# Block-causal attention and two feed-forward layers on one core: the order of weight conversions and token cuts is changed in five places

## The chip, the cores and the metric

The kernel runs on one core of a Trainium2 chip. The metric is the device time of one execution in microseconds (us). Three runs of the kernel before gave 957.68 us in the median (956.08 to 958.67). The engines are named as the profile names them: PE multiplies matrices (PEld loads its weights), DVE and ACT do elementwise work, POOL helps in attention, SP issues DMAs. Each engine works through its own instructions in the order in which they were written.

## The reference

```python
# q, k, v: (4, 8, 576, 64); 2304 tokens of 512 after the heads are joined
scores = scale * q @ k^T;  mask by blocks of 64 (block_i >= block_j)
attn = softmax(scores);    x = (attn @ v), heads joined -> (2304, 512)
g = relu(x @ w_in) ** 2;   x = g @ w_out          # first layer, 512 -> 2048 -> 512
h = x @ w_in2;  g = h * cos(h);  out = g @ w_out2  # second layer, same sizes
```

## The kernel before, in words

**Number format.** Every fp32 operand of the two layers is held as two parts, "high" (the value rounded, made by ACT) and "low" (the rest, made by DVE from the value and the high part). A product of two such operands is three matmuls: high by high, high by low, low by high. Tokens are cut in this way by a copy and a subtraction. Weights come from DRAM as 64-bit words, and the class `Half` converts half a chunk (512 KB: a chunk's in-weights, h = 0, or its out-weights, h = 1) by eight instructions: on ACT `shift`, `rebias`, `high`, on DVE `mask`, `join`, `sign`, `power`, `low`. A call of `convert()` finishes one half, begins the next and asks SP to load a further one. The list `loads` sets the order of the halves.

**Stages.** Attention fills `xall` with all tokens. The order of its instructions is made by a planner, which also places the conversion of two halves (EARLY) and the cut of the first 512 tokens. The first layer then begins with a block of 768 tokens (512, and 256 beside them), in a loop over the 16 chunks of the hidden dimension, `first_block`: the hidden product of chunk c (24 matmuls), a conversion, ACT's activation of the chunk, its gs parts, a second conversion, and the output product of chunk c-1 (24 matmuls). The hidden product of chunk 1 is put into the banks `accs[3]` and `hs[3]`, which the output product of chunk 0 writes as its last ones. The in-weights are also written back to DRAM, and come again as "streams" (`ws`) for later blocks.

Three blocks of 512 tokens follow in the first layer (`first_layer`, eight steps r of two chunks each), and in the second layer four blocks of 512 tokens (`second_layer`, eight steps each) and a last one of 256 (`last_block`). A step's output matmuls are put in the list `pend`, and `pop` places them between later products, so that PE has work while DVE and ACT prepare the next operands.

**Second layer.** A hidden product is split into quarters and made from seven smaller products (42 matmuls of 256 columns), named by the weight part and the token part: 11 by 11, s2 by t2, s1 by t1, 12 by 21, s3 by t3, 22 by t4, s4 by 22. Their sums are taken on ACT (`copy`, into p1 and c11) and DVE (`plus`). The activation h·cos(h) of a step runs in pieces: `count`, `less`, `rest`, `size` at the step's end, `size`, `cosine`, `times`, `high`, `low` in the next step. For every block the tokens' quarters and their sums are prepared during the block before (`prepare`): four sums on DVE, and seven cuts, of which those of "11" and "t2" are the last. They are also the first two that the next block's products read. `prepared(n)` emits n of these items.

What the change touches: the sort key of `loads` (L234), the streams' ranges in `stream` (L827), the list that `prepare` returns (L974), the pops at the end of the first layer's last step (L1134), and in `second_layer` the places of `convert` and of `prepared` (L1187 to L1215).

Of the kernel before, what the change touches and what calls it, by code (L numbers as in the profile page):

```python
# [175 lines left out]
def tile_block_causal_attention__then__two_ffn(  # L176
# [54 lines left out]
    BESIDE = 256  # L231
    loads = [((layer, c), h) for layer in range(2) for c in range(KF) for h in range(2)]

    loads.sort(key=lambda x: (x[0][0], x[0][1] + (KF if x[0][0] else 1) * x[1], -x[1]))  # L234
    loads.reverse()
    loaded, begun = [], []
    freed, given, done = [0], [], set()
# [509 lines left out]
    def layers():  # L747
# [74 lines left out]
        def stream(s):  # L822
            i, r = steps[s]
            layer = blocks[i][0]
            assert layer == 0 or (layer, r, "sums", 1) in done
            w = ws_p.tile([128, 7 * DM], F32R, tag="ws", name="ws")
            ranges = [(0, 4)] if layer == 0 else [(0, 7)] if i < len(blocks) - 1 else [(0, 3), (7, 8)]  # L827
            at = 0
            for a, z in ranges:
                nc.sync.dma_start(  # L830
                    out=w[:, at * DM : (at + z - a) * DM].bitcast(F32), in_=parts[layer][r][:, a * DM : z * DM]
                )
                at += z - a
            return w
# [113 lines left out]
        def prepare(t0, n, own, room):  # L948

            m = 256  # L950
            src = {}
            def sum_of(name, one, two):
                if name in ("t1", "t2"):
                    tile = room(name == "t2")
                    for x, s in enumerate((name, "t3" if name == "t1" else "t4")):
                        src[s] = tile[:, x].rearrange("p (k n) -> p k n", k=2)[:, :, 0:m]
                nc.vector.tensor_tensor(out=src[name], in0=src[one], in1=src[two], op=ALU.subtract)

            def cut(name):
                to = own[name][:, :, :, 0:m]  # L960
                nc.scalar.copy(out=to[:, 0], in_=src[name])
                nc.vector.tensor_tensor(
                    out=to[:, 1], in0=src[name], in1=to[:, 0].bitcast(F32), op=ALU.subtract
                )

            if n == 256:
                src.update({name: xall[:, k : k + 2, t0 : t0 + n] for name, k in zip(names, (0, 2))})
                return [lambda name=name: cut(name) for name in names[0:2]]
            src.update({
                f"{k + 1}{j + 1}": xall[:, 2 * k : 2 * k + 2, t0 + j * m : t0 + (j + 1) * m]  # L970
                for k in range(2) for j in range(2)
            })
            sums = (("t1", "12", "11"), ("t3", "22", "12"), ("t2", "22", "t1"), ("t4", "21", "t2"))
            return [lambda s=s: sum_of(*s) for s in sums] + [lambda name=name: cut(name) for name in names]  # L974

        u = [x_p.tile([128, 256], F32, name=f"u{n}") for n in range(2)]

        place = {
# [119 lines left out]
        def pop(n):  # L1098
            for _ in range(min(n, len(pend))):
                pend.pop(0)()  # L1100
# [10 lines left out]
        def first_layer(s, i, r):  # L1111

            n, w, gs = blocks[i][2], ws.pop(0), gsb[s % 2]
            for x in range(2):
# [11 lines left out]
                if r < half - 1:  # L1126
                    pop(3 * KD)
                elif x:
                    if i < last:
                        fresh.extend(Cut(*blocks[i + 1][1:], kk) for kk in range(KD))  # L1130
                        for c in fresh:
                            c.high()
                            c.low()
                    pop(6 * KD)  # L1134
                squares(h, x, n, gs)
                if s == 0 and x == 0:
                    for a in range(KD):
# [20 lines left out]
                    prepared(1)  # L1158
            if i == last and r == half - 1:
                prepared(len(todo))  # L1160

        def second_layer(s, i, r):

# [6 lines left out]
            def copy(to, bank):  # L1170
                nc.scalar.copy(out=to, in_=bank[:, 0:m])  # L1171
# [12 lines left out]
            times("s1", "t1", bank_c, True)  # L1184
            times("12", "21", bank_a, False)
            copy(c11, bank_a)
            pop(2 if len(pend) > per else 0)  # L1187
            times("s3", "t3", bank_b, False)
            plus(c22, bank_b, p1)
            plus(c22, bank_c, c22)  # L1190
            run(("high", 1), ("low", 1), ("high", 0), ("low", 0))
            pop(len(pend) - per - 3)
            times("22", "t4", bank_b, False)
            plus(c21, bank_b, p1)
            pop(len(pend) - per)
            times("s4", "22", bank_c, False)
            plus(c12, bank_c, u2)
            late.clear()
            late.update(waves(n, gs, [ha[:, x, 0:n] for x in range(2)]))
            run(("count", 1), ("less", 1), ("count", 0), ("less", 0), ("rest", 1), ("rest", 0), ("size", 1))  # L1200
            ws.append(stream(s + 2))
            if loads or loaded or begun:
                convert()
            elif i + 1 < len(blocks):
                if r >= 1 and not todo and ready[0] < i:
                    ready[0] = i
                    if len(sets) < 2:
                        add_set()
                    todo.extend(prepare(
                        *blocks[i + 1][1:], sets[(i - last) % 2],  # L1210
                        lambda x: raw_p.tile([128, 2, 512], F32, tag="raw", name="t"),
                    ))
                prepared(max(0, min(2, len(todo) - 2)))
                if r == half - 1:
                    prepared(len(todo))  # L1215

        def last_block(s, i, r):

# [91 lines left out]
```

## Time and profile before

| what | us |
|---|---|
| median of three runs | 957.68 |
| the profiled execution | 955.75 |
| its span | 953.9 |
| PE busy in the span | 929.5 (97%) |
| DVE busy | 674.7 (71%) |
| ACT busy | 617.5 (65%) |

A row of the timeline has the start, the length, the engine, the line, the operation, what it writes and reads, and how many instructions were merged; in brackets stands the idle time before it and what ended it. The chain of waits is read in the same way, and a row of it shows the piece of the chain alone. A row of the windows view has the stretch, its length, the busy time of PE, PEld, DVE, ACT and POOL, then the granted TensorE clock as a share of full speed, the share of DMA and GB/s. Where a row's length is that of a group of matmuls, its end is modelled; the start of the next group tells when PE was free.

### The profile page before, as it was taken

The page shows a single profiled execution, that of the slowest core. Times are in us where ns is not written, and L with a number is a line of the kernel's source. Part 1 is how long each engine was busy: PE and PEld are TensorE (multiplying, and loading weights), DVE is VectorE, ACT ScalarE, POOL GpSimd, SP SyncE. Part 2 cuts the span into 40 slices and gives each one's busy share as a digit, 9 for nine tenths or more (in the row PEclk, how much of TensorE's full clock was granted, in tenths as well). Part 3 has the DMA queues.
Part 4 walks back from the last instruction along what each step waited for, and adds up shares of the span by engine and source line. Part 5 has one row for each costly group of instructions (what it writes and reads, how often), then busy time and mean ns, then how long its engine had stood idle before and what let it go on. Part 6 is the DMA issues. An engine that isn't in the chain of part 4 may idle for free.

```text
span 953.9 us, 15725 instructions
## 1 busy us (share of the span) xinstructions
PE 929.5 (97%) x5818; PEld 788.1 (83%) x5818; DVE 674.7 (71%) x1394; ACT 617.5 (65%) x1319; POOL 93.5 (10%) x204
## 2 busy tenths in 40 slices
PE   8999998999999999999999989999999999999998
PEld 4777776888888888888888878988998998998887
DVE  6998997777776556555466678767776876766554
ACT  7987897777886555655567765555555555544554
POOL 4867740000000000000000000000000000000000
PEclk9999999999999999999999999999999999999999
DMA  8444304567654777676555744446544555544272
GB/s 306 152 136 137 118 30 146 167 205 248 197 191 167 273 240 232 232 252 227 193 177 191 274 175 155 155 155 213 200 173 155 203 189 193 197 156 172 72 255 76
DMA packets 40156, 176.12 MB, mean 185 GB/s; under 512 B 4112, under 2 KB 9488, under 8 KB 32912
## 3 DMA queue, kind: packets, MB, share of 16 engines
q1 hardware_dynamic: 39360, 174.41, 52.9%
q8 instruction: 45, 0.74, 0.3%
q10 hardware_dynamic: 720, 0.72, 0.2%
q14 instruction: 31, 0.25, 0.1%
HBM read 145.23 MB, written 29.88 MB: 184 GB/s over the span
## 4 chain that ended last, share of the span: by engine, by line
PE 89%; DVE 4%; ACT 3%; DMA 2%; issue 1%; POOL 0%; ACTq 0%; SPq 0%; DVEq 0%
PE acc L1055 19%; PE h L988 16%; PE h L1119 14%; PE acc L1053 13%; PE h L855 5%; PE ps L656 4%; PE ps L440 4%; PE ps L601 4%; PE acc L879 4%; PE h L879 2%; PE h L1226 2%; DMA raw<-in_w_dram 1%; PE ps L488 1%; DVE g L1011 1%; PE ps L628 1%; DMA ws<-parts1.3_2028 1%
## 5 line engine op out<-in xcount | busy, mean ns | idle before, releaser
L1055 PE MATMUL acc<-w,gs 128*128 128x512 f32 x864 | 220.0, 392 | 0.0
L1055 PEld LDWEIGHTS acc<-w,gs 128*128 128x128 f32 x864 | 154.0, 189 | 25.3
L1053 PE MATMUL acc<-gs,w 128*128 128x512 f32 x576 | 138.3, 389 | 0.0
L1119 PE MATMUL h<-xs,ws 128*128 128x512 f32 x576 | 137.7, 389 | 0.0
L1119 PEld LDWEIGHTS h<-xs,ws 128*128 128x128 f32 x576 | 108.0, 188 | 22.3
L1053 PEld LDWEIGHTS acc<-gs,w 128*128 128x128 f32 x576 | 107.8, 188 | 22.2
L999 DVE TENSOR_TENSOR gs<-ha,gs 128x512 fp32r<-128x512 f32 x48 | 33.2, 692 | 91.7 <-ACT gs L998 91.7
L1008 ACT ACTIVATE turns<-ha 128x512 int32<-128x512 f32 x64 | 40.5, 633 | 73.7 <-DVE ha L1174 73.6
L1016 ACT ACTIVATE g<-g 128x512 f32<-128x512 f32 (+1 forms) x80 | 47.2, 590 | 52.7 <-DVE g L1011 52.7
L988 PE MATMUL h<-w,ws 128*128 128x256 f32 x480 | 70.8, 284 | 2.8 <-ACT u L1171 1.8
L1174 DVE TENSOR_TENSOR ha<-h,u 128x256 f32<-128x256 f32 x96 | 40.6, 423 | 45.3 <-PE h L988 45.2
L988 PEld LDWEIGHTS h<-w,ws 128*128 128x128 f32 x480 | 66.2, 192 | 7.6 <-ACT u L1171 2.2
L855 PE MATMUL h<-xs,w 128*128 128x256 f32 (+1 forms) x372 | 67.3, 336 | 1.2 <-ACT w L307 1.2
L307 ACT CAST w<-bits 128x512 fp32r<-128x512 f32 x64 | 39.9, 624 | 42.1 <-DVE bits L285 42.1
L855 PEld LDWEIGHTS h<-xs,w 128*128 128x128 f32 x372 | 57.9, 190 | 9.3 <-ACT w L307 1.4
L996 ACT ACTIVATE ha<-h 128x512 f32<-128x512 f32 x48 | 28.5, 594 | 52.4 <-PE h L1119 52.4
L1019 ACT ACTIVATE g<-g,half_pi 128x512 f32<-128x512 f32 (+1 forms) x80 | 50.6, 672 | 0.5
L1022 DVE TENSOR_TENSOR g<-ha,g 128x512 f32<-128x512 f32 x64 | 41.7, 692 | 12.0 <-ACT g L1019 11.8
L1028 DVE TENSOR_TENSOR gs<-g,gs 128x512 fp32r<-128x512 f32 (+1 forms) x80 | 47.9, 631 | 2.6 <-ACT gs L1025 2.5
L1011 DVE SCALAR_TENSOR_TENSOR g<-turns,g 128x512 f32<-128x512 int32 (+1 forms) x80 | 48.0, 633 | 0.5
L1011 DVE SCALAR_TENSOR_TENSOR g<-turns,ha 128x512 f32<-128x512 int32 x64 | 44.0, 688 | 5.1 <-ACT turns L1008 5.0
L656 PE MATMUL ps<-PT,vB 128*64 128x320 f32 (+4 forms) x448 | 46.8, 360 | 0.0
(173 smaller groups left out, 1693.3 us busy)
## 6 DMA issues: line engine op xcount, KB each, us to landing
raw<-in_w_dram SPq DMA_DIRECT2D x64, 512.0 KB, 4.4
qB<-in_qd_dram SPq DMA_DIRECT2D x15, 576.0 KB, 5.4
ws<-parts1.0_2025 SPq DMA_DIRECT2D x4, 1792.0 KB, 7.4
ws<-parts1.1_2026 SPq DMA_DIRECT2D x4, 1792.0 KB, 7.2
ws<-parts1.2_2027 SPq DMA_DIRECT2D x4, 1792.0 KB, 7.3
ws<-parts1.3_2028 SPq DMA_DIRECT2D x4, 1792.0 KB, 8.3
ws<-parts1.4_2029 SPq DMA_DIRECT2D x4, 1792.0 KB, 7.4
ws<-parts1.5_2030 SPq DMA_DIRECT2D x4, 1792.0 KB, 7.2
```

The lines of the kernel that those rows point to most:

```text
L656: nc.tensor.matmul(plan.bank(s)[own, a - c0 : c1 - c0], lhsT=vB[x][:, j, e], rhs=PT[:, x, j, e, a:c1], start=(n == 0), stop=(n == len(todo ...
L855: nc.tensor.matmul(h, lhsT=w[:, a, kk * 128 : (kk + 1) * 128], rhs=xs[kk].parts[:, y], start=(m == 0), stop=(m == 3 * KD - 1),)
L879: nc.tensor.matmul(accs[a][:, 0:n], lhsT=w[:, x, a * 128 : (a + 1) * 128], rhs=gs[:, y], start=(c == 0 and m == 0 and a % shared == 0), st ...
L988: nc.tensor.matmul(bank[:, 0:n], lhsT=w[:, c : c + 128], rhs=own[two][:, y, k, 0:n], start=(start and k == 0 and i == 0), stop=(k == 1 and ...
L1011: nc.vector.scalar_tensor_tensor(out=own, in0=turn, scalar=-part, in1=start, op0=ALU.mult, op1=ALU.add)
L1016: nc.scalar.activation(out=own, in_=own, func=AF.Abs)
L1019: nc.scalar.activation(out=own, in_=own, func=AF.Sin, bias=half_pi, scale=-1.0)
L1022: nc.vector.tensor_tensor(out=own, in0=h, in1=own, op=ALU.mult)
L1028: nc.vector.tensor_tensor(out=to[:, 1], in0=own, in1=to[:, 0].bitcast(F32), op=ALU.subtract)
L1053: nc.tensor.matmul(accs[a][:, 0:n], lhsT=w[:, y, sl], rhs=gs[:, z, x, 0:n], **flags)
L1055: nc.tensor.matmul(accs[a], lhsT=gs[:, y, x, sl], rhs=w[:, z], **flags)
L1119: nc.tensor.matmul(h[:, 0:n], lhsT=w[:, c : c + 128], rhs=xs[kk].parts[:, y], start=(m == 0), stop=(m == 3 * KD - 1),)
```

## The change

Five edits. The halves of the first layer's weights come in the order c + 1.5·h, so that the two converted in attention are the in-weights of chunks 0 and 1, and each chunk's out-weights come half a place after the next chunk's in-weights. The cuts of "11" and "t2" are split: both high parts, then both low parts. In the second layer the conversion moves from the step's end to its middle, the high parts of the last two cuts to the middle of the block's last step, and the low parts right behind its last sum. The first layer's last step pops 12 output matmuls instead of 24, and ends with a Sin on one column, which brings ACT's table load there. The last block's streams come in three DMAs instead of two.

```diff
-    loads.sort(key=lambda x: (x[0][0], x[0][1] + (KF if x[0][0] else 1) * x[1], -x[1]))
+    loads.sort(key=lambda x: (x[0][0], x[0][1] + (KF if x[0][0] else 1.5) * x[1]))
...
-            ranges = [(0, 4)] if layer == 0 else [(0, 7)] if i < len(blocks) - 1 else [(0, 3), (7, 8)]
+            ranges = [(0, 4)] if layer == 0 else [(0, 7)] if i < len(blocks) - 1 else [(0, 2), (2, 3), (7, 8)]
...
-            def cut(name):
+            def high(name):
+                nc.scalar.copy(out=own[name][:, 0, :, 0:m], in_=src[name])
+
+            def low(name):
                 to = own[name][:, :, :, 0:m]
-                nc.scalar.copy(out=to[:, 0], in_=src[name])
                 nc.vector.tensor_tensor(
...
+            def cut(name):
+                high(name)
+                low(name)
...
-            return [lambda s=s: sum_of(*s) for s in sums] + [lambda name=name: cut(name) for name in names]
+            return [lambda s=s: sum_of(*s) for s in sums] + [lambda name=name: cut(name) for name in names[0:5]] + [
+                lambda name=name, f=f: f(name) for f in (high, low) for name in names[5:]
+            ]
...
-                    pop(6 * KD)
+                    pop(6 * KD if i < last else 3 * KD)
...
                 prepared(len(todo))
+                nc.scalar.activation(out=scrap, in_=half_pi, func=AF.Sin)
...
             copy(c11, bank_a)
+            if r == half - 1:
+                prepared(2)
             pop(2 if len(pend) > per else 0)
...
             run(("high", 1), ("low", 1), ("high", 0), ("low", 0))
+            if loads or loaded or begun:
+                convert()
             pop(len(pend) - per - 3)
...
             plus(c12, bank_c, u2)
+            if r == half - 1:
+                prepared(len(todo))
...
-            if loads or loaded or begun:
-                convert()
-            elif i + 1 < len(blocks):
+            if not (loads or loaded or begun) and r < half - 1 and i + 1 < len(blocks):
...
-                prepared(max(0, min(2, len(todo) - 2)))
-                if r == half - 1:
-                    prepared(len(todo))
+                prepared(max(0, min(2, len(todo) - 4 * (blocks[i + 1][2] > 256))))
```

The first place is ACT at the beginning of the first layer, where w0 names in-weights, w1 out-weights, h0, h1 and acc3, h3 the banks of the hidden products of chunks 0 and 1. Before:

```order
L307 CAST w1_2000<-bits_1972 128x512
...
L866 CAST gs0_2036<-ha_2033 128x256
L261 ACTIVATE raw_1997<-raw_1997 128x512
L307 CAST w0_2108<-bits_2089 128x512
L274 ACTIVATE bits_2106<-bits_2106,new_bias_59 128x512
L261 ACTIVATE raw_2093<-raw_2093 128x512
L307 CAST w1_2144<-bits_2106 128x512
L274 ACTIVATE bits_2142<-bits_2142,new_bias_59 128x512
L864 ACTIVATE ha_2033<-acc3_2048 128x512
```

And now:

```order
L307 CAST w0_2000<-bits_1972 128x512
...
L866 CAST gs0_2036<-ha_2033 128x256
L261 ACTIVATE raw_1997<-raw_1997 128x512
L307 CAST w1_2108<-bits_2089 128x512
L274 ACTIVATE bits_2106<-bits_2106,new_bias_59 128x512
L261 ACTIVATE raw_2093<-raw_2093 128x512
L307 CAST w0_2144<-bits_2106 128x512
L274 ACTIVATE bits_2142<-bits_2142,new_bias_59 128x512
L864 ACTIVATE ha_2033<-acc3_2048 128x512
```

No instruction has moved: the same places of the conversion now hold other weights, w0_2000 being chunk 1's in-weights, w1_2108 chunk 0's out-weights and w0_2144 chunk 2's in-weights.

The second place is DVE at the end of the first layer (gs1 is the activation of its last step, w1 an out-weight's low part, x11 and xt2 the low parts of the cuts of "11" and "t2", u1 and ha the second layer's sums). Before:

```order
L962 TENSOR_TENSOR x11_4822<-xall_60,x11_4822 128x512
L999 TENSOR_TENSOR gs1_2037<-ha_2033,gs1_2037 128x512
L962 TENSOR_TENSOR xt2_4823<-turns_2035,xt2_4823 128x512
L999 TENSOR_TENSOR gs1_2037<-ha_2033,gs1_2037 128x512
L285 SCALAR_TENSOR_TENSOR bits_5198<-raw_5120,bits_5198 128x512
L268 TENSOR_SCALAR bits_5272<-raw_5162 128x512
L291 TENSOR_SCALAR raw_5120<-bits_5198 128x512
L310 SCALAR_TENSOR_TENSOR w1_5274<-raw_5120 128x512
L279 SCALAR_TENSOR_TENSOR raw_5162<-raw_5162 128x512
L1174 TENSOR_TENSOR u1_3352<-h1_2042,u0_3351 128x256
```

And now:

```order
L1008 TENSOR_TENSOR gs1_2037<-ha_2033,gs1_2037 128x512 x2
L285 SCALAR_TENSOR_TENSOR bits_5199<-raw_5121,bits_5199 128x512
L268 TENSOR_SCALAR bits_5259<-raw_5163 128x512
L291 TENSOR_SCALAR raw_5121<-bits_5199 128x512
L310 SCALAR_TENSOR_TENSOR w1_5261<-raw_5121 128x512
L279 SCALAR_TENSOR_TENSOR raw_5163<-raw_5163 128x512
L964 TENSOR_TENSOR x11_4823<-xall_60,x11_4823 128x512
L964 TENSOR_TENSOR xt2_4824<-turns_2035,xt2_4824 128x512
L1184 TENSOR_TENSOR u1_3353<-h1_2042,u0_3352 128x256
```

Both low parts now stand behind the last gs and behind all five DVE instructions of a conversion.

The third place is DVE at the end of the second block of the second layer (ha are the sums c21 and c12, g with turns the `less` and `rest` of the activation). Before:

```order
L1174 TENSOR_TENSOR ha_2033<-h1_2042,u0_3351 128x256
L1174 TENSOR_TENSOR ha_2033<-h2_2043,u1_3352 128x256
L1011 SCALAR_TENSOR_TENSOR g_2034<-turns_2035,ha_2033 128x512 x2
L1011 SCALAR_TENSOR_TENSOR g_2034<-turns_2035,g_2034 128x512 x2
L962 TENSOR_TENSOR x11_4822<-xall_60,x11_4822 128x512
L962 TENSOR_TENSOR xt2_4823<-t_6315,xt2_4823 128x512
```

And now:

```order
L1184 TENSOR_TENSOR ha_2033<-h1_2042,u0_3352 128x256
L1184 TENSOR_TENSOR ha_2033<-h2_2043,u1_3353 128x256
L964 TENSOR_TENSOR x11_4823<-xall_60,x11_4823 128x512
L964 TENSOR_TENSOR xt2_4824<-t_6317,xt2_4824 128x512
L1020 SCALAR_TENSOR_TENSOR g_2034<-turns_2035,ha_2033 128x512 x2
L1020 SCALAR_TENSOR_TENSOR g_2034<-turns_2035,g_2034 128x512 x2
```

The two low parts have moved ahead of four instructions of the activation.

## Rows read from the trace of the kernel before

**Rows 1.** The page's busy times, share of the span, instructions.
```profile
PE 929.5 (97%) x5818; PEld 788.1 (83%) x5818; DVE 674.7 (71%) x1394; ACT 617.5 (65%) x1319; POOL 93.5 (10%) x204
```
**Rows 2.** Timeline, the first layer's first two chunks.
```profile
150.40 4.45 PE L855 MATMUL h<-xs,w 128*128 128x512 f32 x24
...
158.60 4.46 PE L855 MATMUL acc<-xs,w 128*128 128x512 f32 x12 [3.76 <-ACT w L307]
158.60 0.69 DVE L310 SCALAR_TENSOR_TENSOR w<-raw 128x512 fp32r<-128x512 uint32 x1
...
161.06 0.72 ACT L274 ACTIVATE bits<-bits,new_bias 128x512 int32<-128x512 int32 x1
...
168.52 3.74 PE L855 MATMUL h<-xs,w 128*128 128x512 f32 x19
```
**Rows 3.** Windows, behind two waits of PE.
```profile
158.60:160.60 2.00, 2.00 (x5) 1.56 (x6) 2.00 (x4) 1.22 (x3) 0.00 (x0) 0.50 0.09 20
...
637.50:639.00 1.50, 1.50 (x9) 1.50 (x9) 1.24 (x2) 0.52 (x1) 0.00 (x0) 0.50 0.00 0
```
**Rows 4.** Timeline, PE at chunks 8 and 9.
```profile
218.68 4.34 PE L855 MATMUL h<-xs,w 128*128 128x512 f32 x24
...
228.35 4.78 PE L855 MATMUL h<-xs,w 128*128 128x512 f32 x24 [1.15 <-ACT w L307]
```
**Rows 5.** The chain of waits there.
```profile
213.10 8.68 DMA raw<-in_w_dram
...
237.31 4.18 PE h L855 x24
```
**Rows 6.** Timeline, from the first layer to the second.
```profile
541.75 5.60 PE L1053 MATMUL acc<-gs,w 128*128 128x512 f32 x24
...
543.90 0.69 DVE L999 TENSOR_TENSOR gs<-ha,gs 128x512 fp32r<-128x512 f32 x1 [1.43 <-ACT gs L998]
...
546.59 0.68 DVE L279 SCALAR_TENSOR_TENSOR raw<-raw 128x512 int32<-128x512 int32 x1
...
547.20 0.88 PE L988 MATMUL h<-x,ws 128*128 128x256 f32 x6
...
555.74 0.88 PE L988 MATMUL h<-x,ws 128*128 128x256 f32 x6
...
558.97 1.28 ACT L1019 ACT_TABLE_LOAD   x1
...
567.69 0.88 PE L988 MATMUL h<-x,ws 128*128 128x256 f32 x6
...
571.35 0.98 PE L988 MATMUL h<-w,ws 128*128 128x256 f32 x6 [1.35 <-ACT u L1171]
...
579.82 0.88 PE L988 MATMUL h<-x,ws 128*128 128x256 f32 x6
```
**Rows 7.** Timeline, PE from block 1 to block 2 of the second layer.
```profile
611.46 0.88 PE L988 MATMUL h<-x,ws 128*128 128x256 f32 x6
...
621.99 0.88 PE L988 MATMUL h<-x,ws 128*128 128x256 f32 x6
...
647.01 0.88 PE L988 MATMUL h<-x,ws 128*128 128x256 f32 x6
```
**Rows 8.** Timeline, PE from block 2 to block 3.
```profile
710.17 0.88 PE L988 MATMUL h<-x,ws 128*128 128x256 f32 x6
...
733.09 0.88 PE L988 MATMUL h<-x,ws 128*128 128x256 f32 x6
```
**Rows 9.** Timeline, from block 4 to the last block.
```profile
882.32 0.88 PE L988 MATMUL h<-x,ws 128*128 128x256 f32 x6
...
896.15 4.27 PE L1055 MATMUL acc<-w,gs 128*128 128x512 f32 x18
...
905.89 1.28 SPq L830 DMA_DIRECT2D ws<-parts1.2_2027  x2
...
911.35 3.14 PE L1226 MATMUL h<-w,ws 128*128 128x256 f32 x24 [1.13 <-DMA ws<-parts1.2_2027]
```

More of the change, by code (lines that the diff above doesn't have):

```diff
@@ L973, in prepare @@
             sums = (("t1", "12", "11"), ("t3", "22", "12"), ("t2", "22", "t1"), ("t4", "21", "t2"))
-            return [lambda s=s: sum_of(*s) for s in sums] + [lambda name=name: cut(name) for name in names]
+            return [lambda s=s: sum_of(*s) for s in sums] + [lambda name=name: cut(name) for name in names[0:5]] + [
+                lambda name=name, f=f: f(name) for f in (high, low) for name in names[5:]
+            ]
+        scrap = work.tile([128, 1], F32, name="scrap1")
         u = [x_p.tile([128, 256], F32, name=f"u{n}") for n in range(2)]
```

## The prediction

> **What bounds the kernel now.** I read the page first: PE is busy for 929.5 of 953.9 us [rows 1], so an edit can win only what PE waits, and what it pays behind a wait. Then I listed PE's waits by stretch, and measured each place by the starts of PE's groups in the timeline, because a start tells when PE was free and the modelled ends don't. The reader is to see five places. In the first layer's second chunk PE waits 3.76 for ACT's high part of the in-weights [rows 2]; behind that wait, and behind one in the second layer, the granted clock is 0.50, which is the level of 1.2 GHz [rows 3]. Eight chunks on it waits again, 1.15 [rows 4]. Third, the passage from the first layer to the second [rows 6]. Fourth, the ends of the second layer's blocks [rows 7 to 9]. Fifth, the last block's streams [rows 9]. Between them PE works without a gap, and nothing that DVE or ACT saves there counts.
>
> **The first layer's begin.** Half a chunk is 4.18 [rows 5], so the hidden products of chunks 0 and 1 and the output product of chunk 0 are 12.54, and chunk 2 would start at 150.40 + 12.54 = 162.94. It starts at 168.52 [rows 2]: 5.58 lost, 3.76 as the wait and the rest by the slow clock behind it. Now chunk 1's in-weights are ready. The wait for them goes, and two others are next. Chunk 0's out-weights take their place in the conversion, with the low part ready at 158.60 + 0.69 = 159.3 [rows 2]; PE wants it at its third matmul behind 158.76: a tenth or two. And the output product's fourth quarter overwrites the bank that holds chunk 1's hidden product. ACT must read that first, but its activation is queued behind the second conversion, whose last instruction ends at 161.06 + 0.72 [rows 2]; with some 0.6 for the activation the bank is free at 162.4. PE, at 0.23 for a matmul of 512 columns (5.45 for 24 from the starts in [rows 6]), gets there at 161.0: a wait of 1.4, too short for the slow clock by the one of 1.35 in [rows 6], whose group of six takes 0.98 where others take 0.88. Gain 5.58 - 1.5 = 4.1; bounds 2.5 (the slow clock comes after all) and 5.6.
>
> The later wait: from 218.68 to 237.31 [rows 4, 5] are two chunks, 16.72 of work in 18.63, so 1.9 lost. A load of raw weights took 8.68 there [rows 5], and the chunk's second conversion, which must finish the next chunk's in-weights before PE turns to them, came late. Now the first conversion finishes them, ahead of the activation, and the second one has until PE ends the next hidden product, 4.18 later. A delay of 1.9 fits into that. Gain 1.9; bounds 0 and 1.9.
>
> **From the first layer to the second.** What it loses now: PE goes on at 547.20 and passes 579.82 three steps later [rows 6], 32.6. A full step is 10.53 [rows 7] and the first of these holds 12 output matmuls fewer, half of 547.20 - 541.75 = 5.45; so the work is 3 x 10.53 - 2.72 = 28.9, and 3.7 is lost. The edits do three things there. The Sin moves the table load of 1.28 [rows 6] into a stretch where ACT waits for PE: nothing on the path. Twelve output matmuls go between the products, so PE reaches the first product at 541.75 + 2.72 = 544.5. But the low part of "11", which its second matmul reads, now stands behind a conversion. DVE's gs starts at 543.90 and the conversion's last instruction ends at 547.27 [rows 6]; 0.69 of that is the gs, 2.7 the conversion. The low part follows, ready at 547.9. PE waits 3.4 where it waited nothing, and pays the slow clock as in [rows 2]: there 8.36 of work from 158.60 took until 168.52, so 1.56. Together 5.0.
>
> The conversion in mid-step: it holds DVE for 2.7 ahead of the sums c21 and c12, so the activation's start, and with it the copy of p1 behind it on ACT's queue, come that much later; against that p1 no longer stands behind ACT's part of a conversion at the step's end, which made the wait of 1.35 [rows 6]. I went through the steps queue by queue with the lengths in the trace. Step 0 converts nothing, as the out-weights it would overwrite are still to be read. In step 1 the copies of the first layer's last results stand behind the conversion, and PE's next output matmuls wait about 1.0 for their banks; step 2 loses nothing, step 3 about 0.8, step 4 a tenth. So 6.9 in all, 3.2 more than now. Bounds: the first wait without slow clock and no more, 3.4, a gain of 0.3; all of 5.0 and 2.7 in each of three conversions, 13.1, a loss of 9.4. I take the middle way because the row that is nearest, the step from 567.69, loses 1.6 with a conversion on the path.
>
> **The blocks' ends.** From 621.99 to 647.01 are two steps [rows 7]: 25.02 for 21.06, so 3.96 lost, part of it slow clock [rows 3]. PE waits for the cut of "11", made after the activation's pieces. Now both low parts stand before these pieces and are ready when PE gets there; they push the activation by 1.2, and p1 has about as much room in the next step. At this one boundary the preparation starts late, so an entire cut falls into the middle of the step, ahead of the sums on DVE, and costs 0.8. Gain 3.1. From 710.17 to 733.09 [rows 8]: 22.92, 1.86 lost, and one more boundary like it; gain 3.7 for both. Into the last block: from 882.32 to 896.15 [rows 9] are a step and 12 matmuls of 256 columns at 0.12 (42 of them and 24 long ones make the step); 13.83 for 11.98, and both cuts are now made in the step r = 1; gain 1.85. Bounds for all three terms: 4 (the activation pushed back takes half) and 9.7.
>
> **The last streams.** PE was free at 911.35 - 1.13 = 910.2, the DMA of 768 KB was issued at 905.89 [rows 9]. Its first 512 KB suffice for the first half of the product. They land between two thirds of 5.4 and all of it, 909.5 to 911.3; the second half's parts still land about 912, when PE wants them at 911.6 or so. Gain 0.7; bounds -0.5 and 1.1.
> The page "DMA: Bandwidth & Descriptors" of the Trainium skill speaks against a third DMA: its section on the anatomy of one DMA gives each about 2.0 us of fixed cost, and its rules for kernel authors ask for 1 MiB or more in one. The row shows two DMAs issued within 1.28 and both in by 911.35, less than the sum of two separate ones would need, so the trace bears the rule out only in part. By the page's figure the last part of each stream would land 2.0 later, an estimate of 4.0 us lost in two steps.
>
> **Sum.** 4.1 + 1.9 - 3.2 + 3.1 + 3.7 + 1.85 + 0.7 = 12.15. The profiled execution, 955.75, becomes 943.6; the median of the runs is 1.93 above it, and 957.68 - 12.15 gives 945.5.
>
> **Rivals.**
> - The passage between the layers goes by its bad bound, 9.4 lost: 945.5 + 6.2 = 951.7. For it: three conversions on a DVE that is fullest there. Against: only one of three steps loses more than 1.5 now. Chance 0.14.
> - The passage costs nothing more than now: 945.5 - 3.2 = 942.3. It needs DVE to be early, which its order denies. Chance 0.1.
> - The change doesn't remove the first wait but hands it on: PE waits as long for chunk 0's out-weights or the bank. Then 4.1 goes: 949.6. For it: the conversions stand where they stood. Against: their times above. Chance 0.07.
> - A stream's parts pay one after the other: the third one adds a third of the 5.4, 1.8, before the product's second half, in this step and the next, which both wait for their streams: 3.6 lost instead of 0.7 won, 949.8. For it: SP issues them one by one. Against: two land together now. Chance 0.04. The page's rule above is this one.
> - Slower: out-weights late in every chunk. They now come out of the second conversion, with the next hidden product as their only cover. If conversions and gs need more than 8.36 a chunk, each of 14 chunks loses the excess; from 1.1 a chunk on the 12.15 and the 0.3% are gone, at 1.5 it is 945.5 + 21 = 966.5. Against: two conversions of 2.7 on DVE and some 1.1 of gs are 6.5. Chance 0.03.
>
> The forecast has the remaining 0.62. Its own range with the small bounds is 943 to 948. The range of 940.5 to 951.5 leaves out the slower rival, half of the bad passage, and the best of all bounds. A measurement of this kernel tells 0.3% (2.9 us) from no change: faster needs 954.8 or less, which every case but the last gives; for what I haven't seen I leave 0.03 to no change and 0.03 to slower.
>
> **What would show it.** Right: PE's second chunk starts without a wait for weights, with one of 1 to 1.5 at the fourth bank; no wait at chunk 9; a wait of about 3.4 on DVE's low part of the cut at the second layer's first product, and the clock at 0.50 behind it; steps across a block's end of 10.5 to 11.3. Wrong: the slow clock in the first layer's begin; output matmuls there that wait for DVE's low part of the weights; no wait at the second layer's first product; block ends that lose over a microsecond.

## The result and the profile after

The changed kernel takes 944.26 us, median of 4 runs (942.30 to 946.10), beside 956.88 for the kernel before: ratio 0.9866, interval 0.9834 to 0.9898. Forecast were 945.5, in 940.5 to 951.5. A second series gave 943.83 (943.0 to 944.7), ratio 0.9857 [0.9842, 0.9872]. The profiled execution took 942.58, its span is 940.8.

First the page's busy line of the kernel after, which answers [rows 1]:

```profile
PE 924.4 (98%) x5818; PEld 785.7 (84%) x5818; DVE 673.3 (72%) x1394; ACT 615.4 (65%) x1320; POOL 93.6 (10%) x204
```

The span is 13.1 shorter, PE's busy time 5.1. Busy time shrinks without a matmul less because a matmul at the low clock counts as busy for longer (twelve of 256 columns take 2.29 from start to start behind the wait of 3.18 below, 1.40 a step later), and for one more reason, which the run with a pad finds below.

By the starts of PE's groups, before and after (us):

| stretch | before | after | gained | forecast |
|---|---|---|---|---|
| up to the first hidden product | 150.40 | 150.65 | -0.25 | 0 |
| to chunk 2 | 18.12 | 14.33 | 3.79 | 4.1 |
| the other chunks, to the first product of the next block | 118.79 | 116.58 | 2.21 | 1.9 |
| first layer's other blocks | 254.44 | 254.44 | 0.00 | 0 |
| last group of the first layer to the second layer's sixth step | 59.18 | 62.16 | -2.98 | -3.2 |
| to the last step of block 4 (three block ends) | 281.39 | 273.58 | 7.81 | 6.8 |
| into the last block | 13.83 | 11.92 | 1.91 | 1.85 |
| last block | 46.90 | 46.16 | 0.74 | 0.7 |

The rest of the 13.1 is -0.13 at the end. Timeline of the kernel after (start, duration, engine, line, out<-in, in brackets the idle time before and its releaser), first chunks and chunks 8 to 10, beside [rows 2, 4]:

```profile
150.65 4.42 PE L855 MATMUL h<-xs,w 128*128 128x512 f32 x24
...
161.32 0.72 ACT L274 ACTIVATE bits<-bits,new_bias 128x512 int32<-128x512 int32 x1
161.94 0.57 ACT L864 ACTIVATE ha<-acc 128x512 f32<-128x512 f32 x1
...
162.57 0.97 PE L879 MATMUL acc<-gs,w 128*128 128x512 f32 x3 [1.07 <-ACT ha L864]
...
164.98 4.31 PE L855 MATMUL h<-xs,w 128*128 128x512 f32 x24
...
214.94 4.31 PE L855 MATMUL h<-xs,w 128*128 128x512 f32 x24
218.78 0.68 ACT L261 ACTIVATE raw<-raw 128x512 uint32<-128x512 uint32 x1 [3.79 <-DMA raw<-in_w_dram]
223.27 4.31 PE L855 MATMUL h<-xs,w 128*128 128x512 f32 x24
231.60 4.31 PE L855 MATMUL h<-xs,w 128*128 128x512 f32 x24
```

The 3.76 are gone. The fourth bank is waited for, 1.07, and its releaser is ACT's activation, which starts when the conversion's last instruction is out of ACT's queue. Chunks 8 to 10 now stand 8.33 apart. The load of raw weights is still late there, ACT waits 3.79 for it, but PE no longer does.

The passage between the layers, beside [rows 6]:

```profile
536.00 2.88 PE L1062 MATMUL acc<-gs,w 128*128 128x512 f32 x12
538.15 0.69 DVE L1008 TENSOR_TENSOR gs<-ha,gs 128x512 fp32r<-128x512 f32 x1 [2.03 <-ACT gs L1007]
538.72 0.28 PE L997 MATMUL h<-x,ws 128*128 128x256 f32 x1
540.78 1.28 ACT L1170 ACT_TABLE_LOAD   x1
540.84 0.68 DVE L279 SCALAR_TENSOR_TENSOR raw<-raw 128x512 int32<-128x512 int32 x1
541.44 0.68 DVE L964 TENSOR_TENSOR x<-xall,x 128x512 fp32r<-128x512 f32 x1
542.18 0.85 PE L997 MATMUL h<-x,ws 128*128 128x256 f32 x5 [3.18 <-DVE x L964]
...
554.18 0.86 PE L997 MATMUL h<-x,ws 128*128 128x256 f32 x6
...
562.86 3.20 PE L1064 MATMUL acc<-w,gs 128*128 128x512 f32 x12 [0.79 <-ACT xall L1079]
565.89 0.86 PE L997 MATMUL h<-x,ws 128*128 128x256 f32 x6
```

PE gets one matmul in and then waits 3.18 for the low part of "11", which stands on DVE behind the conversion that ends at 541.52. The first step takes 15.46 where a full one takes 10.48. The windows (us, then busy time of PE, PEld, DVE, ACT and POOL, granted clock, DMA share, GB/s) at the fourth bank and behind this wait, beside [rows 3]:

```profile
161.00:162.60 1.60, 0.53 (x4) 0.09 (x2) 1.56 (x4) 1.57 (x4) 0.00 (x0) 1.00 0.72 266
542.20:543.50 1.30, 1.30 (x10) 1.30 (x11) 0.53 (x1) 0.45 (x2) 0.00 (x0) 0.88 0.69 173
543.50:545.00 1.50, 1.50 (x9) 1.50 (x9) 0.42 (x1) 0.00 (x0) 0.00 (x0) 0.50 0.60 227
```

Around the wait of 1.07 the clock stays at its upper level, 2.4 GHz. After the one of 3.18 it falls to 0.50, 1.2 GHz.

The block ends 1 to 2 and 2 to 3, and the last streams, beside [rows 7 to 9]:

```profile
619.11 0.86 PE L997 MATMUL h<-x,ws 128*128 128x256 f32 x6
...
625.59 0.97 PE L997 MATMUL h<-w,ws 128*128 128x256 f32 x6 [0.71 <-DVE ha L1184]
...
630.55 0.86 PE L997 MATMUL h<-x,ws 128*128 128x256 f32 x6
...
704.00 0.86 PE L997 MATMUL h<-x,ws 128*128 128x256 f32 x6
714.50 0.86 PE L997 MATMUL h<-x,ws 128*128 128x256 f32 x6
...
893.49 1.70 SPq L830 DMA_DIRECT2D ws<-parts1.2_2027  x3
...
898.67 1.56 PE L1238 MATMUL h<-w,ws 128*128 128x256 f32 x11 [0.94 <-DMA ws<-parts1.2_2027]
```

The step across the end of block 1 is 11.44; across the end of block 2 it is 10.50, a step like any other. The last block still waits for a stream. Its DMAs (KB each, median us from issue to landing):

```profile
ws<-parts1.2_2027 SPq DMA_DIRECT2D x1, 512.0 KB, 5.1
ws<-parts1.2_2027 SPq DMA_DIRECT2D x2, 256.0 KB, 5.3
```

### The profile page after: what moved, and what is told of

Read it like the earlier page. It is cut to its first block, busy times and chain, and to the rows that moved or that the text cites. A ratio compares the mean times of both kernels' runs of the same rounds, so it can differ in the third digit from the quotient of the medians.

```text
span 940.8 us, 15737 instructions
## 1 busy us (share of the span) xinstructions
PE 924.4 (98%) x5818; PEld 785.7 (84%) x5818; DVE 673.3 (72%) x1394; ACT 615.4 (65%) x1320; POOL 93.6 (10%) x204
## 4 chain that ended last, share of the span: by engine, by line
PE 91%; DVE 4%; ACT 2%; DMA 2%; issue 0%; POOL 0%; SPq 0%; ACTq 0%; DVEq 0%; POOLq 0%
PE acc L1064 19%; PE h L997 16%; PE h L1128 14%; PE acc L1062 13%; PE h L855 6%; PE acc L879 4%; PE ps L601 4%; PE ps L440 4%; PE ps L656 4%; PE h L879 2%; PE h L1238 2%; PE ps L488 1%; DMA kB<-in_kT_dram 1%; PE ps L628 1%; DMA ws<-parts1.2_2027 1%; DVE g L1020 0%
## 5 line engine op out<-in xcount | busy, mean ns | idle before, releaser
L1062 PE MATMUL acc<-gs,w 128*128 128x512 f32 x576 | 138.9, 389 | 0.0
L1031 DVE TENSOR_TENSOR g<-ha,g 128x512 f32<-128x512 f32 x64 | 41.8, 692 | 13.1 <-ACT g L1028 13.1
L879 PE MATMUL acc<-gs,w 128*128 128x512 f32 x192 | 47.0, 392 | 1.1 <-ACT ha L864 1.1
```

What stands on the lines that cost most here:

```text
L879: nc.tensor.matmul(accs[a][:, 0:n], lhsT=w[:, x, a * 128 : (a + 1) * 128], rhs=gs[:, y], start=(c == 0 and m == 0 and a % shared == 0), st ...
L1031: nc.vector.tensor_tensor(out=own, in0=h, in1=own, op=ALU.mult)
L1062: nc.tensor.matmul(accs[a][:, 0:n], lhsT=w[:, y, sl], rhs=gs[:, z, x, 0:n], **flags)
```

## The experiments

"The change" below is the changed kernel. Each run stands beside the kernel before on the same chip. Differences between two edited kernels are taken from their traces, and where from ratios, this is said.

**The two kernels again.** No edit.

> The changed kernel once more, beside the kernel before on one chip. Theory A (the edits explain it all): ratio 0.987, within 0.003, and an ordinary step of the second layer 10.53 us in both profiles. Theory B (part of the difference between the two profiles is a pace of the run: a step of 10.48 after against 10.53 before, a chunk of 8.33 against 8.36, steps of the first layer 10.88 in both): the changed kernel's steps go with the run and not with the edits, and the ratio comes nearer to 0.989, since the sum of the places that the edits touch is 11.0 to 11.5 and not 13.1.

> The kernel before, profiled on the same chip as the run above. Theory A: steps of 10.53 us and chunks of 8.36 as in its first profile, while the changed kernel on this chip shows 10.48. Theory B: both kernels show the same step on this chip, whichever of the two it is.

Measured: 943.83, and 957.82 for a single run of before. A second-layer step is 10.48 in the one and 10.53 in the other, a chunk 8.33 and 8.36: the pace belongs to the kernel, not to the run. The wait of 3.17 was the same, but the first step of the second layer took 16.48 this time, 1.0 more than in the trace above, with the clock at 0.50 for longer.

**The order of the loads alone**, in the kernel before:

```diff
-loads.sort(key=lambda x: (x[0][0], x[0][1] + (KF if x[0][0] else 1) * x[1], -x[1]))
+loads.sort(key=lambda x: (x[0][0], x[0][1] + (KF if x[0][0] else 1.5) * x[1]))
```

> The kernel before with the one line that sorts the loads as in the change. Theory A (the terms of the sum stand for themselves): 5.7 us less than before (3.8 at the second chunk, 1.9 at chunk 9), ratio 0.994; the wait of 3.76 gone, one of about 1.1 at the fourth bank. Rival (DMA or conversion only push the loss on to a later chunk, and the rest of the change gave the gain): within 2 us of before, with a wait of PE in a chunk after the second.

Measured: 951.28, ratio 0.9936 [0.9923, 0.9948], 6.2 less. From the first hidden product to the next block's first it took 131.38 for 136.95, so 5.57, and the chunks' pace stayed 8.36. PE's row at the fourth bank is that of the change:

```profile
165.13 0.96 PE L879 MATMUL acc<-gs,w 128*128 128x512 f32 x3 [1.07 <-ACT ha L864]
```

So one line of the change carries both of its gains in the first layer's begin.

**The first set's cuts in one piece**, high and low part together; later sets as in the change:

```diff
+if len(sets) < 2:
+    return [lambda s=s: sum_of(*s) for s in sums] + [lambda name=name: cut(name) for name in names]
```

> The changed kernel, but the first set of token cuts (made in the first layer's last block) is not split: each low part comes right behind its high part, as before. Theory A (the wait of 3.2 us at the second layer's first product and the slow clock behind it are caused by the low part standing behind a conversion): no wait there, clock 1.00, 4.7 to 5.0 us less than the changed kernel, so about 939.5 where that has 944.3. Rival (PE, earlier by that, then waits as long for the sums, the conversions or the banks of the first layer's results in the next steps): less than 2 us gained, the step with the copies of these results longer by what was won.

Measured: 941.23, ratio 0.983 [0.9813, 0.9847]. The first step takes 12.36 for 15.46, so 3.1 come back and not 4.7 to 5.0. How much it is hangs on the clock behind the wait in the execution it is compared with: beside the 13.9 of two runs below, where the clock stayed up, it would be 1.5, beside the 16.48 above 4.1; the medians of the two kernels on this chip differ by 2.6. The timeline shows what PE still loses:

```profile
540.71 1.28 ACT L1172 ACT_TABLE_LOAD   x1
...
542.11 0.35 ACT L1183 COPY u<-h 128x256 f32<-128x256 f32 x1
...
542.52 0.98 PE L999 MATMUL h<-w,ws 128*128 128x256 f32 x6 [1.61 <-ACT u L1183]
```

PE has no more wait for the low part and reaches its next one at 540.91. The copy of p1 that it needs there stands on ACT behind the table load. In the change this load lies in PE's wait and costs nothing; without the wait it is on the path.

**All 24 output matmuls ahead of the second layer's first product**, as before:

```diff
-pop(6 * KD if i < last else 3 * KD)
+pop(6 * KD)
```

> The changed kernel with all 24 output matmuls placed ahead of the second layer's first product, as before. Theory A (the twelve that were put between the products brought PE 2.7 us earlier to a low part that was not ready, and fill the first step's small waits of 0.5 to 1): the wait for the low part is 3.2 - 2.7 = 0.5, the slow clock doesn't come, so 1.6 + 2.7 are won at the product and some 2 to 2.7 lost in the first step, which lacks its filler: 1.5 to 2 us faster than the changed kernel. Rival (the filler is worth what it covers): same or slower.

Measured: 941.33, ratio 0.9838 [0.9816, 0.986]. The output matmuls fill the wait:

```profile
539.28 5.60 PE L1062 MATMUL acc<-gs,w 128*128 128x512 f32 x24
544.72 0.28 PE L997 MATMUL h<-x,ws 128*128 128x256 f32 x1
545.45 0.86 PE L997 MATMUL h<-x,ws 128*128 128x256 f32 x5 [0.45 <-DVE x L964]
...
563.72 3.19 PE L1064 MATMUL acc<-w,gs 128*128 128x512 f32 x12 [1.26 <-ACT xall L1079]
```

From the first layer's last block to the sixth step it took 313.42, with the cuts in one piece 313.50, before 313.62, in the change 316.60. Either edit gives the passage back what the change took from it, here 3.2 where 1.5 to 2 were expected; about 1.5 of that is the slow clock in the change's trace. The wait is what cost, and it takes both, the split cut and the early product, to make it. Block 1's last step takes 10.47 here, for 11.44 in the change: the conversions end in the second layer's third step and not in its fourth, so the preparation starts a step earlier and no entire cut is left for that last step.

**The conversion back at the step's end.**

```diff
 run(("high", 1), ("low", 1), ("high", 0), ("low", 0))
-if loads or loaded or begun:
-    convert()
 ...
 ws.append(stream(s + 2))
-if not (loads or loaded or begun) and r < half - 1 and i + 1 < len(blocks):
+if loads or loaded or begun:
+    convert()
+elif r < half - 1 and i + 1 < len(blocks):
```

> The changed kernel with the conversions of the second layer's first steps back at the step's end; all else as changed. Theory A (either place costs about the same: in the middle DVE's sums wait for it, at the end ACT's copy of p1): the three steps behind the first lose 2 to 3 us in all, as the 2.0 of the changed kernel (1.2, 0.05, 0.8): 0 to 1 us slower than the changed kernel. Rival 1 (the middle is worse, as the sums start the next activation): 1 us faster or more. Rival 2 (the middle is what wins): 2 us slower or more.

Measured: 942.81, ratio 0.9856 [0.9832, 0.988]. The second to fifth steps take 43.77 at the end and 43.98 in the middle. The place makes no difference that counts in the sum. The waits are others: that for ACT's copies of the first layer's last results, 0.79 in the change (562.86), is gone, and PE waits 0.52 and 0.71 for the copy of p1.

**The block ends as before**, first with the split lists left in. In this kernel the high parts of "11" and "t2", whose tiles the sets share, are overwritten while the block still reads them, that of "11" at the end of its sixth step and that of "t2" at the end of its seventh (699.89 and 711.66 in block 2), so the last two steps of blocks 2 and 3 compute with other tokens.

> The changed kernel with the preparation of the next block's tokens back at the end of the block's last step, behind the activation's pieces; the list stays split. Theory A (the block ends are worth 3.0 + 1.86 + 1.86 + 1.9): 8.5 us slower than the changed kernel, waits of 1 to 2 us at the four blocks' first products, and the slow clock behind the first. Rival (the order in the step matters little, and the ends gained by the pace of the run): less than 4 us slower.

Measured: 957.03, ratio 0.9991 [0.9976, 1.0006]. Around the end of block 2 PE waits three times (700.56, in the step ahead of the last, 1.52 for ACT's part; 712.32, 0.30; 723.40, in the next block's first step, 0.91 for DVE's): here the split itself puts waits ahead of the end, so this doesn't price the place. With the lists of the second and later sets in one piece as well:

```diff
+if len(sets) >= 2:
+    return [lambda s=s: sum_of(*s) for s in sums] + [lambda name=name: cut(name) for name in names]
 ...
-if r == half - 1:
-    prepared(2)
 ...
-if r == half - 1:
-    prepared(len(todo))
 ...
-if not (loads or loaded or begun) and r < half - 1 and i + 1 < len(blocks):
+if not (loads or loaded or begun) and i + 1 < len(blocks):
 ...
-prepared(max(0, min(2, len(todo) - 4 * (blocks[i + 1][2] > 256))))
+prepared(max(0, min(2, len(todo) - 2)))
+if r == half - 1:
+    prepared(len(todo))
```

> The changed kernel with the blocks' ends alone as before: the preparation runs at the end of the step again, in the last step too, and from the second set on each cut is one entry (its low part right behind its high part), so that no shared tile is written a step early. Theory A (the cut of "11" behind the activation's pieces is what PE waits for at a block's end): from the start of the sixth step of the second layer to the last block 283.6 - 1.1 for the faster pace = 282.5 instead of 273.6, minus what the last step's two cuts cost there; 952.4 for 943.8, with waits for the cut of "11" of 1.5 to 3.5 at the first products of three blocks. Theory B (the split of the cuts matters and the place of the preparation does not): below 947.5. Both keep the step of 10.48.

Measured: 949.93, ratio 0.9936 [0.9917, 0.9956], by the ratios 7.6 more than the change. From the sixth step to block 4's last 278.81 for 273.58, and 2.25 from there to the end: 7.5. The waits stand where theory A wants them:

```profile
629.65 0.39 PE L999 MATMUL h<-x,ws 128*128 128x256 f32 x1 [1.51 <-ACT x L960]
630.46 0.85 PE L999 MATMUL h<-x,ws 128*128 128x256 f32 x5 [0.42 <-DVE x L964]
```

They are 1.5 and 0.4, and 1.0 and 0.35 at the three other ends. Against the 8.6 forecast 1.1 are missing. The end of block 1 explains that: its two steps take 23.43 here and 25.03 in the second run of before. The waits are the same, and the pace is 0.1 of the 1.6; before, the clock is at 0.50 behind them [rows 3], here it is not:

```profile
542.10:543.50 1.40, 1.40 (x12) 1.40 (x13) 0.55 (x1) 0.48 (x2) 0.00 (x0) 1.00 0.78 184
543.50:545.00 1.50, 1.50 (x15) 1.50 (x14) 0.42 (x1) 0.00 (x0) 0.00 (x0) 1.00 0.60 224
630.00:632.00 2.00, 1.58 (x14) 1.54 (x14) 1.00 (x2) 0.77 (x3) 0.00 (x0) 1.00 0.76 323
```

The first two windows stand behind the same wait of 3.18 as in the change, and there too the clock stayed up: 13.92 for the first step instead of 15.46.

**Two DMAs for a stream of the last block.**

```diff
-[(0, 2), (2, 3), (7, 8)]
+[(0, 3), (7, 8)]
```

> The changed kernel with the last block's streams in two DMAs, as before. In the changed kernel the 512 KB that come first landed 5.1 us after their issue, and PE still waited 0.94. Theory A (all parts of a stream land nearly together, so the split gives little): within 0.5 us of the changed kernel, a wait of 1.1 and one of 0.4. Theory of the prediction (the first part lands earlier and frees the product's first half): 0.7 us slower. Rival (a third DMA has its price): 1 us faster.

Measured: 945.46, ratio 0.9879 [0.9856, 0.9902], which overlaps with the change's. From block 4's last step to the end it took 65.87, in the change 65.07, in four other traces with three DMAs 65.11 to 65.28: the split is worth 0.6 to 0.8. PE waits 0.94 for this stream as in the change, where 768 KB take 5.2 and the split parts took 5.1 and 5.3; nothing is won there. It waits 0.61 for the next stream (906.09), where the change waits nothing. That stream's first DMA in the change and in this run:

```profile
ws<-parts1.3_2028 SPq DMA_DIRECT2D x1, 512.0 KB, 6.1
```

```profile
ws<-parts1.3_2028 SPq DMA_DIRECT2D x1, 768.0 KB, 6.9
```

So here the split brings its first part in 0.8 sooner, at 904.36 in the change, when PE wants it at 904.38. It does so too in the streams that PE doesn't wait for: the last three take 4.0 to 4.1 with 512 KB and 4.5 to 4.6 with 768. Why the stream waited for gains only 0.1 is open.

**A pad.** The kernel before with the change's new tile, which nothing reads, and nothing else; its pool lies ahead of xs2, x11, xt1 and xt2, which move by 32 bytes (so do the sums u, which PE doesn't read):

```diff
+scrap = work.tile([128, 1], F32, name="scrap1")
```

> The kernel before, with one unused tile of 128x1 more in the pool that stands ahead of the tiles xs2, x11, xt1 and xt2, as the change has it for its scrap; no instruction is added or moved, only those tiles lie 32 bytes further on. Theory A (the place of the moving operand sets the faster pace): a second-layer step of 10.48 for 10.53 and a first-layer chunk of 8.33 for 8.36, groups of six matmuls on x and xt at 0.86 for 0.88; 16 x 0.03 + 33 x 0.045 = 2.0 less than the kernel before, all its waits unchanged. Theory B (the faster pace comes with what the engines beside PE do now): 10.53 and 8.36, no difference in time.

Measured: 955.22, ratio 0.9984 [0.9969, 0.9999]: 2.2 less by the medians, 1.5 [0.1, 3.0] by the ratio. The steps are 10.48, the chunks 8.33. Second layer, PE, the second run of before and the pad:

```profile
659.74 0.88 PE L988 MATMUL h<-x,ws 128*128 128x256 f32 x6
660.45 0.88 PE L988 MATMUL h<-xt,ws 128*128 128x256 f32 x6
661.17 0.88 PE L988 MATMUL h<-w,ws 128*128 128x256 f32 x6
```

```profile
658.99 0.86 PE L989 MATMUL h<-x,ws 128*128 128x256 f32 x6
659.69 0.86 PE L989 MATMUL h<-xt,ws 128*128 128x256 f32 x6
660.39 0.88 PE L989 MATMUL h<-w,ws 128*128 128x256 f32 x6
```

Six matmuls on the moved tiles take 0.70 from start to start for 0.72, those on w as long as before. Theory A holds: no instruction is other than before.

**The waits that the change leaves, taken away together.** To the cuts in one piece come four edits:

```diff
 # Sin behind the first copy of c11 instead of at the first layer's end
+if i == last + 1 and r == 0:
+    nc.scalar.activation(out=scrap, in_=half_pi, func=AF.Sin)
 # chunk 1: activation, then the second conversion
-convert()
+if c != 1:
+    convert()
 for f in (act, low, act2, low2):
     f()
+if c == 1:
+    convert()
 # last block: stream(s + 2) right behind the last hidden product of a step
+if x and s + 2 < len(steps):
+    ws.append(stream(s + 2))
 # second layer: convert() one product later
```

> The changed kernel with five edits: the first set's cuts in one piece, the Sin moved behind the first copy of c11 in the second layer's first step, chunk 1's activation ahead of the second conversion, the last block's streams issued right behind the last hidden product, and the conversion of the second layer one product later. Theory A (the four waits left by the change are each worth their length): 3.1 (cuts in one piece, measured) + 1.3 (the table load out of the way of the copy of p1) + 1.0 (wait at the fourth bank) + 0.9 (wait for the last stream) + 0.2 = 6.5 less than the changed kernel, 937.3. Theory B (a wait taken away is handed on to the next engine in the row): only the measured 3.1, 940.7.

Measured: 937.31 (935.4 to 938.19), ratio 0.9792 [0.9774, 0.981], the fastest kernel of this study; by the ratios 6.2 less than the change. By the traces 7.2:

- The first four steps of the second layer take 44.53 for 48.96, so 4.4, near the 4.6 hoped for from three edits; 1.5 of it is the slow clock in the change's trace. 1.50 are still lost in the third step for the copy of p1.
- Fifth step to block 4's last 283.08 for 284.06: the 0.95 at block 1's end have gone. The conversions end a step earlier here, in the third, as in the run with all 24 output matmuls ahead, which lost nothing at that end either.
- Block 4's last step to the end 63.80 for 65.07, 1.3: the stream's issue no longer stands behind the output's DMA on SP's queue, and PE doesn't wait.
- The first chunks gain 0.4 and not 1.0. The wait is handed on, as theory B says:

```profile
163.44 4.70 PE L855 MATMUL h<-xs,w 128*128 128x512 f32 x24 [0.57 <-ACT w L307]
```

- Chunks 8 and 9 lose 0.64. PE's matmuls show no wait there, but its weight loads do, 0.25 for ACT's activation (222.32) and 0.46 for the low part of out-weights. Both are late because ACT waited for a load of raw weights, which landed at 219.97 where in the change it landed at 218.78, and what stands behind it on ACT's queue is as much later (the next conversion begins at 224.66 for 223.47); why the load landed later isn't shown:

```profile
219.97 0.71 ACT L261 ACTIVATE raw<-raw 128x512 uint32<-128x512 uint32 x1 [4.47 <-DMA raw<-in_w_dram]
...
227.28 2.11 PEld L879 LDWEIGHTS acc<-gs,w 128*128 128x128 f32 x10 [0.46 <-DVE w L310]
```

- The attention ended 0.7 earlier, which no edit touches.

The sum is near theory A's 6.5, but not by its terms alone: 0.95 came at a place that it didn't name, the chunks gave nothing in the end, and the attention's 0.7 is chance.

**More pads.** The same kernel, with the tiles xs, y, yt and gs moved by pads so that they too begin 32 bytes off a multiple of 64 (the other tiles behind the first pads move by 128 bytes or more):

> As the kernel with the five edits, and with unused tiles of 128x1 that put the token tiles of the first pool (xs, and y and yt in the second layer) and the activation tiles gs 32 bytes further on; xs2, x11, xt1 and xt2 stay where the change has them. Theory A (256-column matmuls go faster with the moving operand at such a place): in the second and fourth blocks of the second layer three groups of six matmuls take 0.70 from start to start for 0.72, so 0.06 a step, 16 steps: 1.0 less; first-layer steps stay at 10.88. Theory C (512-column matmuls too): the first-layer step falls below 10.85 and the time by 2 to 4. Theory B (the place has nothing to do with it): same time and steps as without.

Measured: 947.76, ratio 0.9906 [0.989, 0.9922], 10.5 more by the medians. All three theories fall. No new wait shows. Twelve matmuls of 512 columns take 2.79 from start to start, without the pads 2.72:

```profile
330.56 2.96 PE L1071 MATMUL acc<-gs,w 128*128 128x512 f32 x12
333.35 2.96 PE L1137 MATMUL h<-xs,ws 128*128 128x512 f32 x12
```

```profile
331.50 2.88 PE L1067 MATMUL acc<-gs,w 128*128 128x512 f32 x12
334.22 2.88 PE L1133 MATMUL h<-xs,ws 128*128 128x512 f32 x12
```

The second fence is the kernel with the five edits. The 256-column ones on gs went from 119 to 117 ns each, as theory A says, but those on x and xt went back from 117 to 120, though their offset from a multiple of 64 is the same: these pads had carried them on by 192 bytes. So the place sets the pace, the 512-column ones lose where the 256-column ones may win, and the rule behind it is open.

## Why the prediction was right

- **First layer's begin** (forecast 4.1 + 1.9). Right in place and size: 1.07 at the fourth bank for an estimated 1.4, without the slow clock; 3.79 gained, and 5.57 for both terms with the loads alone. Chunk 0's out-weights cost PE 0.2, the "tenth or two" of the prediction (nine matmuls at 159.05 take 2.44, nine elsewhere 2.23); in no other chunk did they come late. The 1.9 was read a little high: 237.31 is a piece of the chain, the group itself starts at 237.15, so 1.75 was lost there; of the 2.21 gained 0.4 is pace.
- **Passage** (-3.2). Right: a wait of 3.18 for an estimated 3.4, the first step 4.98 longer for 5.0; the steps behind lost 1.2, 0.05, 0.8 and 0 for 1.0, 0, 0.8 and 0.1. Two parts of the reasoning hold only in part. The 1.56 for the slow clock are one draw of several, and that this one came in the profiled execution is luck: behind the same wait of 3.2 the slow clock cost nothing in two runs (13.91 and 13.92 for the first step), about 1.5 in three (15.46 in the profiled one, 15.37, 15.44) and 2.6 in the second series (16.48). And the steps' losses are not a price of mid-step over the step's end: with the conversion at the end they come to 1.85 for 2.06, in other waits.
- **"Nothing on the path"** for the table load. Right only under the new wait, which covered it. Its cost with that cover gone, of which the prediction said nothing, showed in the run with the cuts in one piece: PE waits 1.61 for the copy behind it.
- **Block ends** (3.1 + 3.7 + 1.85). Right: 0.95 left at block 1's end for 0.8, with a wait of 0.71 for DVE's sums, as reckoned (so that step, 11.44, lies just above the 10.5 to 11.3 named as the sign), nothing at the others; 9.7 gained in the stretches, of which about 1.2 is the pace (27 steps by 0.045). The clean undoing gives 7.1 of the 8.65 back at the four ends, and 0.4 behind them; the missing 1.5 is the clock that fell behind block 1's end before and not here.
- **Last streams** (0.7). The size was right, 0.6 to 0.8 by the run with two DMAs, but not at the stream that the prediction reckoned with. Its first 512 KB came near the late bound, 5.1 after issue, where the whole 768 KB take 5.2, and PE still waits 0.94. The gain came at the next stream, whose 512 KB land after 6.1 where 768 KB take 6.9: the wait of 0.61 is gone. The rival of parts that pay one after the other fails by the rows: the last parts took 5.3 from their issue, 0.2 longer than the first and not 1.8. The section on the anatomy of one DMA in the Trainium skill, "DMA: Bandwidth & Descriptors", gives a DMA issued from GpSimd a fixed cost of about 2.0 us. Here SP issues, and with 5.1 and 5.3 a further DMA in a stream doesn't land 2.0 later: the three overlap.
- **Not foreseen:** the pace. The new tile moves four groups of tiles that PE reads by 32 bytes, worth 1.5 to 2.2 by the pad alone and about 1.8 in the change's trace (14 chunks by 0.03, some 31 steps by 0.045). Without it the trace's 13.1 would be 11.3, 0.85 below the sum of 12.15: that the forecast came within 1.2 of the measured median owes something to a term that wasn't in it.

## What to carry to other kernels

Look for the instruction that stands behind the moved one on its queue: here a wait of 3.2 arose because a cut's low part was put behind a conversion, and the table load was free only while it lasted. When a wait is removed, name the next in line and move that too: five small edits at the places the trace named gave a further 6 us. And when a kernel's every matmul becomes a little faster or slower without a wait, compare where its tiles lie before you explain it by the order of work.

## What the runs showed of the hardware

- Matmuls of 256 columns took 117 or 120 ns each, of 512 columns 227 or 233, by where in SBUF the tiles lie that they read; a shift of the tiles behind one pad by 32 bytes was worth 1.5 us [0.1, 3.0], a second set of pads cost 10.5. Which offsets are good is open.
- Behind the same wait of 3.2 the granted clock fell to 0.50 in four runs (first step 15.37 to 15.46 in three, 16.48 in one) and stayed at 1.00 in two (13.91, 13.92). The wait is sure, its clock isn't.
- Three DMAs of one stream, issued by SP one behind the other, took 5.1 (512 KB) and 5.3 us (256 KB each) from their issue to landing; a part of 512 KB landed 0.1 to 1.3 us sooner than one of 768 KB in the run with two.
- The start of the first hidden product, behind an attention without edits, lay between 149.9 and 153.9 in the profiles. A difference of two single executions below some 3 us is not to be read without the stages.
